# A new order for the pair stage of a spectral mix and gated feed-forward kernel, set by a planner that lets VectorE and POOL take whole turns in SBUF

## The chip, the core and the metric

The kernel runs on one core of a Trainium2 chip. The metric is the device time of one execution in microseconds; the time before is the median of 3 runs, 2704.79 us (2703.63 to 2707.28). The engines are named as in the profile: PE is TensorE, DVE is VectorE, ACT is ScalarE, POOL is GpSimd, SP is SyncE, which here only issues transfers.

## What is computed

```python
# x: 8 x 3008 x 256;  w_r, w_i: 256 x 256;  gate, val: 256 x 1536;  w_out: 1536 x 256
X = np.fft.rfft(x, axis=1)
Yr = Xr @ w_r - Xi @ w_i + b_r
Yi = Xr @ w_i + Xi @ w_r + b_i
Y = soft(Yr) + 1j * soft(Yi)          # soft: sign(v) * max(|v| - 0.01, 0)
y = np.fft.irfft(Y, n=3008, axis=1).reshape(24064, 256)
out = (sigmoid(y @ w_gate) * (y @ w_val)) @ w_out
```

## The kernel before

Every large product is made of three matmuls of parts (high by high, high by low, low by high), so an operand is split into two tiles: ACT writes the rounded part, DVE subtracts it from the value. The transforms and the first columns of the feed-forward end about 1021 us into the profiled execution. What follows to the end is the **pair stage**, the only part that the change touches. It has 19 pairs of column blocks. For each pair it makes both feed-forward products with seven block products in place of eight (Strassen's scheme in Winograd's form), whose intermediate sums are kept in PSUM.

In the code, `half` makes one half (gate or value) of one feature pair: seven products, each of three matmuls of 512 columns (`products`, L1155), into the banks `z`, `c` and `b`. The bank `z` gathers four of the products one after the other, and between two of them ACT copies it out (L1246): a product into `z` must wait for that copy. DVE adds the copies to `b` or `c` (L1249), ACT makes the sigmoid (L1265), and DVE or POOL multiplies gate by value into the tile `h` (L1285, L1287, L1289 on DVE, L1293 on POOL). The multiplication of L1287 frees a `c` bank.

Once three feature pairs are done, `second` makes the output products from `h` into `l2z` banks, again with seven products (of three times three matmuls), again with copies between products (L1351). Its operands are: POOL's differences of slices of `h` (L1320), two sums that a transfer adds into `h` in place (`h<-h`, L1314, issued by POOL, each in two runs of two slices and of one), and the splits of these into tiles `op` (ACT L1331, then DVE L1333). `prepare` loads and splits the next pair's inputs (L1198, L1206, L1207, with POOL's sums at L1211 to L1217). SP issues the loads of weights, `w1s` (L1187, 896 KB, one each half) and `w2s` (L1342, 384 KB, one each product of `second`), and the stores.

The order is a list. Each step is a `Task` with an engine, a duration, a due time and the tasks that it waits for. The due time is the place in a regular scheme plus a number of the table `NUDGE`, one number for each step of each function. `arrange` plays the tasks through a small model of the five engines and the two transfer queues: of the tasks that are ready within `WINDOW` the one with the least due time goes next, and the order in which tasks start there is the order in which the instructions are issued on every engine. On the chip each engine runs its own list strictly in that order. In the model before, a DVE and a POOL step that are both marked `lock` (they work in SBUF alone) run beside each other, each slowed:

```python
both = all(e in busy and busy[e][0].lock for e in SHARED)
rate = {e: SHARED[e] if both and e in SHARED else 1.0 for e in busy}
...
pace = {e: QUEUES[e][0] if len(moving) > 1 else 1.0 for e in moving}
```

Of the kernel before, what the change touches and what calls it, by code (L numbers as in the profile page):

```python
# [112 lines left out]
class Task:  # L113

    def __init__(self, eng, dur, at, fn, deps=(), lat=0.0, lock=False):
# [8 lines left out]
        35.88, 211.51, 46.34, -80.66, 89.38, -188.31, -183.87, 12.03, -179.91, -49.65, -108.66, 69.66, -418.39,  # L124
        -6.25, 526.82, -36.25, 63.45,
    ),
    "half1": (
        30.21, -172.94, -428.44, -29.43, -62.2, -353.59, -143.83, -35.84, -15.75, -266.09, -177.94, -36.82,
        12.27, -36.43, 24.32, -384.25, -231.44,
    ),  # L130
    "last": (
# [5 lines left out]
    ),  # L137
    "load": (
        -3.03,
    ),  # L140
    "prepare": (
        -160.17, 129.89, 132.59, -42.29, -163.88, 148.86, -247.4, 18.25, -9.94, 184.26, 160.89, -45.82, 144.56,
        487.85, -161.32, 91.98, 68.39, -293.04, 78.88,
    ),
# [7 lines left out]
    ),  # L152
# [12 lines left out]
SHARED = {"DVE": 0.47, "POOL": 0.8}  # L165
QUEUES = {"SP": (0.57, 2.06), "POOL": (0.33, 2.48)}
# [9 lines left out]
def arrange(tasks):  # L176
# [3 lines left out]
    queues = {e: [] for e in QUEUES}  # L180
    busy = {}
    for i, t in enumerate(tasks):
# [17 lines left out]
    while len(order) < len(tasks) or busy:  # L200
        wake = []
        for e, ts in waiting.items():
# [15 lines left out]
        step = min(wake + [busy[e][1] / rate[e] for e in busy] + [m[1] / pace[e] for e, m in moving.items()])  # L218
        now += step
        for e, m in moving.items():  # L220
            m[1] -= step * pace[e]
            if m[1] <= 1e-9:
                queues[e].pop(0)
                done(m[0], now + QUEUES[e][1])
        for e in ENGINES:
            if e not in busy:
                continue
            busy[e][1] -= step * rate[e]
            if busy[e][1] > 1e-9:
                continue  # L230
            t = busy.pop(e)[0]
            t.end = now
            if t.lat:
                queues[e].append([t, t.lat])
            else:
                done(t, now)
    return order
# [3 lines left out]
def tile_fft_mix_ffn(ctx: ExitStack, tc, x, w_r, w_i, b_r, b_i, w_one, w_out, mf, mi, mis, fa, ft, out):  # L241
# [866 lines left out]
    def task(eng, dur, at, fn, reads=(), writes=(), lat=0.0, lock=False, deps=()):  # L1108
# [74 lines left out]
    def load_weights(k):  # L1183
# [3 lines left out]
                           lambda: nc.sync.dma_start(t.get().bitcast(F32), td[k // 2 % NH, k % 2]), writes=[t], lat=2.7)  # L1187

    def prepare(p):
# [5 lines left out]
        def part(i, j):  # L1195
# [3 lines left out]
            y.get().rearrange("p t a n -> p t (a n)"), yd[:, :, p * 2 * HW:(p + 1) * 2 * HW]), writes=[y], lat=2.7)  # L1199
# [293 lines left out]
```

## Time and profile before

| what | value |
|---|---|
| median of 3 runs | 2704.79 us (2703.63 to 2707.28) |
| the profiled execution's own time | 2710.75 us |
| its span, from the first to the last instruction | 2708.9 us |
| PE busy over the span | 2662.7 us, 98%, 16763 matmuls |
| DVE, ACT, POOL busy | 79%, 62%, 39% |
| TensorE clock granted over the span | 0.994 of full speed |
| HBM read and written | 440.50 MB and 116.13 MB |

The profiled execution took 5.96 us more than the median of the runs; its rows are used for differences, and these are set against the median. An idle time in the views is the time that an engine stood still before an instruction, with the instruction or transfer that ended it. Since each engine runs its list in order, an instruction that waits holds all those behind it.

### The profile page before, as it was taken

What the parts mean: (1) busy time and instruction counts of PE and PEld (TensorE: products, weight loads), DVE (VectorE), ACT (ScalarE), POOL (GpSimd) and SP (SyncE); (2) the same over time, 40 slices, a digit from 0 to 9 for tenths busy, and PEclk for the clock granted to TensorE, in tenths of its full rate; (3) what the DMA queues carried; (4) which work ended last, traced back from release to release, by engine and by line L of the source; (5) the groups of instructions that cost most, each with busy time, mean ns of one, the idle gap of its engine ahead of it and who ended that gap; (6) DMA issues with size and microseconds to landing.
All of it is one profiled execution on the core that took longest, in us unless ns stands there. A gap on an engine that the chain in (4) does not pass through costs nothing.

```text
span 2708.9 us, 45080 instructions
## 1 busy us (share of the span) xinstructions
PE 2662.7 (98%) x16763; PEld 2178.5 (80%) x16763; DVE 2140.7 (79%) x3100; ACT 1670.5 (62%) x2852; POOL 1055.0 (39%) x963
## 2 busy tenths in 40 slices
PE   9999999999999999999999999999999999999999
PEld 6778888888888878878788788878788788887877
DVE  5778888687789537888888888888888788888876
ACT  4565554545444446676677766766667667776665
POOL 1441012132235013544555445444554455544532
PEclk9999999999999999999999999999999999999999
DMA  9987655677666675878877888787877788787874
GB/s 294 293 285 197 193 151 168 204 208 208 179 185 179 171 218 164 251 237 251 263 238 246 251 246 265 236 247 237 256 249 242 234 269 239 244 259 243 259 227 135
DMA packets 257659, 617.82 MB, mean 228 GB/s; under 512 B 26464, under 2 KB 130656, under 8 KB 257440
## 3 DMA queue, kind: packets, MB, share of 16 engines
q1 hardware_dynamic: 222720, 521.29, 58.5%
q0 software_dynamic: 34608, 93.60, 16.2%
q8 instruction: 133, 2.18, 0.3%
q14 instruction: 86, 0.70, 0.1%
q10 hardware_dynamic: 112, 0.04, 0.0%
HBM read 440.50 MB, written 116.13 MB: 205 GB/s over the span
## 4 chain that ended last, share of the span: by engine, by line
PE 62%; DMA 14%; DVE 10%; ACT 6%; POOL 4%; issue 3%; SPq 0%; DVEq 0%; POOLq 0%; ACTq 0%
PE z L1155 15%; PE l2z L1155 13%; DMA h<-h 11%; PE c L1155 7%; PE pm L447 4%; PE b L1155 3%; PE pb L413 2%; POOL t L1320 2%; PE pia L524 2%; PE pg L577 2%; ACT op L1331 1%; PE pg L578 1%; POOL h L1320 1%; PE po L605 1%; PE pv L577 1%
## 5 line engine op out<-in xcount | busy, mean ns | idle before, releaser
L1155 PE MATMUL z<-xop,w1s 128*128 128x512 f32 x2592 | 684.3, 391 | 11.4 <-ACT tmp L1246 11.1
L1155 PE MATMUL l2z<-op,w2s 128*128 128x512 f32 x2331 | 599.8, 392 | 3.9 <-DMA w2s<-sd 1.9
L1155 PEld LDWEIGHTS z<-xop,w1s 128*128 128x128 f32 x2592 | 484.9, 188 | 123.8 <-ACT tmp L1246 24.0
L1155 PEld LDWEIGHTS l2z<-op,w2s 128*128 128x128 f32 x2331 | 436.2, 188 | 108.2 <-ACT tmp L1351 7.4
L1246 ACT COPY tmp<-z 128x512 f32<-128x512 f32 x684 | 394.3, 584 | 183.1 <-PE z L1155 175.2
L1333 DVE TENSOR_TENSOR op<-h,op 128x1024 fp32r<-128x1024 f32 (+1 forms) x444 | 472.2, 1078 | 24.9 <-ACT op L1331 19.5
L1331 ACT CAST op<-h 128x1024 fp32r<-128x1024 f32 (+1 forms) x444 | 366.4, 837 | 176.1 <-DMA h<-h 100.1
L1155 PE MATMUL c<-xop,w1s 128*128 128x512 f32 x1296 | 362.1, 392 | 5.1 <-DVE h L1287 3.3
L1293 POOL TENSOR_TENSOR h<-tmp 128x512 f32<-128x512 f32 x114 | 180.1, 1580 | 379.6 <-DVE tmp L1249 362.6
L1155 PEld LDWEIGHTS c<-xop,w1s 128*128 128x128 f32 x1296 | 242.7, 188 | 62.8 <-DVE h L1287 10.5
L1249 DVE TENSOR_TENSOR tmp<-tmp,c 128x512 f32<-128x512 f32 x342 | 231.5, 681 | 62.9 <-ACT tmp L1246 41.2
L1320 POOL TENSOR_TENSOR t<-h 128x512 f32<-128x512 f32 x111 | 173.3, 1562 | 158.0 <-DVE h L1285 158.0
L1265 ACT ACTIVATE tmp<-tmp 128x512 f32<-128x512 f32 x342 | 210.3, 632 | 28.4 <-DVE tmp L1249 28.4
L1314 POOL DMA_DIRECT2D h<-h x148 | 128.3, 900 | 165.8 <-DVE h L1289 56.0
L447 PE MATMUL pm<-w_sb,xsh 128*128 128x256 f32 x1008 | 184.4, 285 | 0.0
L1155 PE MATMUL b<-xop,w1s 128*128 128x512 f32 x648 | 182.3, 390 | 0.0
L447 PEld LDWEIGHTS pm<-w_sb,xsh 128*128 128x128 f32 x1008 | 152.9, 189 | 1.0 <-ACT xsh L429 0.4
L1320 POOL TENSOR_TENSOR h<-h 128x512 f32<-128x512 f32 x111 | 148.9, 1341 | 8.7
L458 ACT CAST yh<-yc 128x512 fp32r<-128x512 f32 x84 | 52.2, 621 | 147.0 <-DVE yc L437 146.9
L1155 PEld LDWEIGHTS b<-xop,w1s 128*128 128x128 f32 x648 | 121.3, 188 | 26.0 <-DVE tmp L1249 0.5
L447 PE MATMUL pm<-w_sb,xsl 128*128 128x256 f32 x504 | 139.6, 277 | 0.0
L585 DVE TENSOR_TENSOR sg<-sg,pv 128x512 f32<-128x512 f32 x108 | 74.1, 686 | 74.2 <-PE pv L579 56.0
(199 smaller groups left out, 4933.0 us busy)
## 6 DMA issues: line engine op xcount, KB each, us to landing
w1s<-td SPq DMA_DIRECT2D x228, 896.0 KB, 6.3
w2s<-sd SPq DMA_DIRECT2D x259, 384.0 KB, 4.3
h<-h POOLq DMA_DIRECT2D x74, 512.0 KB, 6.2
zf<-zd SPq DMA_DIRECT2D x96, 256.0 KB, 3.5
vf<-vd SPq DMA_DIRECT2D x128, 192.0 KB, 4.0
vd<-vz SPq DMA_DIRECT2D x84, 256.0 KB, 2.7
ypair<-yd SPq DMA_DIRECT2D x19, 1024.0 KB, 7.4
out_dram<-acc SPq DMA_DIRECT2D x76, 256.0 KB, 4.3
```

What stands on the lines that cost most here:

```text
L447: nc.tensor.matmul(o, l, r, start=(i == 0), stop=(i == len(mms) - 1))
L577: nc.tensor.matmul(t, wh, yth[:, ct], start=(ct == 0), stop=False)
L585: nc.vector.tensor_mul(h, sg, pv)
L1155: nc.tensor.matmul(o, ws[i], vs[j], start=first and not i and not j, stop=i == 1, skip_group_check=not first)
L1246: return t, on("ACT", 0.59, at, lambda: a_.copy(t.get(), z.get()), [z], [t], deps)
L1249: return on("DVE", 0.67, at, lambda: add(t.get(), s.get(), o.get()), [x for x in (s, o) if x is not t], [t], deps)
L1265: return on("ACT", 0.635, at, lambda: a_.activation(t.get(), (o or t).get(), AF.Sigmoid), [o] if o else [], [t], deps)
L1293: made[3, q] = on("POOL", 1.3, 16, lambda: g_.tensor_mul(at_h(3), g22.get(), v.get()), [g22, v], [h], [d22, e22], True)
L1314: return [[on("POOL", 0.9, at + q0, lambda q0=q0, q1=q1: g_.dma_start(h.get()[:, dst, q0:q1], h.get()[:, src, q0:q1], accum_op=ALU.add), [ ...
L1320: return [[on("POOL", 1.3, at + q, lambda q=q: g_.tensor_sub(v()[:, q], h.get()[:, a, q], h.get()[:, b, q]), [h], [o], sum((d[q] for d in ...
L1331: hi = on("ACT", 0.19 + 0.43 * n, at - 8 + q0, lambda q0=q0, q1=q1: a_.copy(t.get()[:, 0, q0:q1], v()[:, q0:q1]), [t_in], [t], sum((d[i] f ...
L1333: lo.append([on("DVE", 0.13 + 0.555 * n, at - 5 + q0, lambda q0=q0, q1=q1: sub(t.get()[:, 1, q0:q1], v()[:, q0:q1], t.get()[:, 0, q0:q1]), ...
```

## The change

The planner's model and the table are changed; no instruction, shape, tile, buffer count or dependence is. Steps that are marked `lock` now run in three phases: 0.147 us in which they run freely, then a wait until the other engine's locked step is done, then the rest. In the queue model each transfer has a length and the share that POOL's transfer gets beside it. The durations of a few steps move by 5 to 15 ns. All numbers of `NUDGE` are new (266 of them); the kernel issues the same instructions in another order.

```diff
 NUDGE = {
     "half0": (
-        35.88, 211.51, 46.34, -80.66, 89.38, -188.31, -183.87, 12.03, -179.91, -49.65, -108.66, 69.66, -418.39,
+        81.78, 197.28, 91.73, -117.95, -250.83, -257.61, -224.48, -163.05, -290.05, -136.01, -349.76, 195.94,
...
-SHARED = {"DVE": 0.47, "POOL": 0.8}
-QUEUES = {"SP": (0.57, 2.06), "POOL": (0.33, 2.48)}
+BEFORE_LOCK = 0.147
+LANDING = {"SP": 2.08, "POOL": 2.13}
+BOTH = 0.848
+W1_LOAD, Y_LOAD, W2_LOAD, OUT_STORE, P_LOAD = (2.58, 0.27), (2.74, 0.39), (1.14, 0.41), (0.83, 0.32), (1.08, 0.6)
+ADDING = (1.82, 0.0), (0.97, 0.0)
...
-            busy[e] = [t, t.dur]
+            busy[e] = [t, BEFORE_LOCK if t.lock else t.dur, 1 if t.lock else 3]
...
-        both = all(e in busy and busy[e][0].lock for e in SHARED)
-        rate = {e: SHARED[e] if both and e in SHARED else 1.0 for e in busy}
         moving = {e: q[0] for e, q in queues.items() if q}
-        pace = {e: QUEUES[e][0] if len(moving) > 1 else 1.0 for e in moving}
+        pool = moving["SP"][0].lat[1] if len(moving) > 1 else 0.0
+        pace = {e: 1.0 if len(moving) < 2 else pool if e == "POOL" else BOTH - pool for e in moving}
...
+            t, _, phase = busy[e]
+            if phase == 1:
+                busy[e] = [t, t.dur - BEFORE_LOCK, 2]
+                continue
+            busy.pop(e)
+            if e in holds:
+                holds.remove(e)
...
+        for e in ENGINES:
+            if e in busy and busy[e][2] == 2 and not holds:
+                busy[e][2] = 3
+                holds.append(e)
```

What the new table makes of the lists is shown at three places. Line numbers of the changed kernel are 14 higher here (L1249 is L1263 there, and so on).

The first is DVE in the second pair, where `second` starts: `op<-t` are splits of POOL's differences in SBUF, `h<-z` and `h<-c` are products of gate and value, and `c<-tmp,c` is the sum that the latter needs. Before:

```order
L1285 TENSOR_TENSOR h<-z,tmp 128x512
L1333 TENSOR_TENSOR op<-t_13922,op 128x1024
L1333 TENSOR_TENSOR op<-t_13922,op 128x512
L1249 TENSOR_TENSOR c<-tmp,c 128x512
L1287 SCALAR_TENSOR_TENSOR h<-c,tmp 128x512
L1249 TENSOR_TENSOR tmp<-tmp,c 128x512
```

The same place in the changed kernel:

```order
L1299 TENSOR_TENSOR h<-z,tmp 128x512
L1347 TENSOR_TENSOR op<-t_13919,op 128x1024
L1263 TENSOR_TENSOR tmp<-tmp,c 128x512
L1263 TENSOR_TENSOR c<-tmp,c 128x512
L1301 SCALAR_TENSOR_TENSOR h<-c,tmp 128x512
L1263 TENSOR_TENSOR tmp<-tmp,c 128x512
L1347 TENSOR_TENSOR op<-t_13919,op 128x512
```

The split of one slice, which stood right ahead of `c<-tmp,c`, now stands four rows later, behind `h<-c`.

The second is ACT in the third pair, around the second of two single casts of `h`: the one that splits a slice into which a transfer has added (`xop` are the next pair's inputs). Before:

```order
L1246 COPY tmp<-z 128x512
L1331 CAST op<-h 128x512 x2
L1206 CAST xop<-s2f 128x512
L1265 ACTIVATE tmp<-z 128x512
L1246 COPY tmp<-z 128x512
L1331 CAST op<-h 128x1024
```

The same place in the changed kernel:

```order
L1345 CAST op<-h 128x512
L1260 COPY tmp<-z 128x512 x2
L1345 CAST op<-h 128x512
L1260 COPY tmp<-z 128x512
L1220 CAST xop<-s2f 128x512
L1279 ACTIVATE tmp<-tmp 128x512 x2
L1345 CAST op<-h 128x1024
```

Two copies of `z` have moved ahead of that cast, and the next copy stands right behind it in place of three rows later.

The third is PE in the fourth pair, two products of one half into one `z` bank (the number behind a name tells the tile, x3 is one product). Before:

```order
L1155 MATMUL z_15279<-xop_15357,w1s_15166 128x512 x3
L1155 MATMUL l2z_15353<-op_15190,w2s_15185 128x512 x3
L1155 MATMUL z_15385<-xop_14638,w1s_15198 128x512 x3
L1155 MATMUL c_15396<-xop_15292,w1s_15198 128x512 x3
L1155 MATMUL z_15279<-xop_15317,w1s_15166 128x512 x3
```

The same two products in the changed kernel:

```order
L1169 MATMUL z_15257<-xop_15337,w1s_15139 128x512 x3
L1169 MATMUL c_15278<-xop_14483,w1s_15119 128x512 x3
L1169 MATMUL l2z_15353<-op_15203,w2s_15190 128x512 x3
L1169 MATMUL z_15257<-xop_15293,w1s_15139 128x512 x3
```

Three products stood between the two before, two stand there now.

## Rows read from the trace of the kernel before

**Rows 1.** Busy time of the engines by stretch, from the start of the pair stage to the end, and in two short stretches: start and end in us, length, busy us of each engine with its count of instructions, granted TensorE clock, share of the DMA engines, GB/s.
```profile
core 0: us, PE busy (x) PEld busy (x) DVE busy (x) ACT busy (x) POOL busy (x), PEclk, DMA share, GB/s
1021.20:2708.90 1687.70, 1663.20 (x7210) 1348.97 (x7208) 1378.99 (x1818) 1155.96 (x1930) 814.22 (x609) 1.00 0.78 240
...
2129.00:2138.00 9.00, 6.82 (x23) 5.12 (x22) 5.53 (x8) 4.31 (x7) 3.54 (x2) 0.81 0.56 172
2612.00:2622.00 10.00, 7.55 (x20) 5.69 (x21) 5.97 (x6) 2.48 (x6) 3.79 (x3) 0.66 0.52 146
```

**Rows 2.** PE in order of time near 1046 us, five products in a row: start us, us, what (128 x 512 outputs, three matmuls), and the stage's end.
```profile
1044.96 0.84 PE L1155 MATMUL z<-s,w1s 128*128 128x512 f32 x3
1045.64 0.84 PE L1155 MATMUL b<-a,w1s 128*128 128x512 f32 x3
...
1048.36 0.84 PE L1155 MATMUL z<-a,w1s 128*128 128x512 f32 x3
...
2701.96 2.88 PE L1155 MATMUL l2z<-op,xop 128*128 128x512 f32 x12
2704.88 0.69 DVE L1444 TENSOR_TENSOR acc<-acc,l2z 128x512 f32<-128x512 f32 x1 [2.03 <-PE l2z L1155]
```

**Rows 3.** Waits of PE's weight loads in the pair stage, whole: who waited for what, us in total, times, longest us.
```profile
PEld z L1155 <- ACT tmp L1246: 24.0, 32, 2.6
PEld c L1155 <- DVE h L1287: 10.7, 18, 0.6
PEld l2z L1155 <- ACT tmp L1351: 7.4, 15, 0.8
PEld l2z L1155 <- DMA w2s<-sd: 7.0, 17, 1.1
PEld c L1155 <- DVE tmp L1249: 2.2, 1, 2.2
PEld l2z L1155 <- DVE acc L1364: 1.4, 4, 0.5
PEld l2z L1155 <- ACT op L1331: 1.1, 1, 1.1
PEld l2z L1155 <- DVE op L1333: 0.7, 1, 0.7
PEld b L1155 <- DVE tmp L1249: 0.5, 2, 0.4
PEld b L1155 <- issue: 0.5, 2, 0.3
PEld z L1155 <- DMA w1s<-td: 0.4, 1, 0.4
```

**Rows 4.** The engines in order of time in the second pair, 1143.9 to 1150.9 us: start us, us, engine and what, idle time before it and what ended it.
```profile
1143.93 0.69 DVE L1285 TENSOR_TENSOR h<-z,tmp 128x512 f32<-128x512 f32 x1 [0.41 <-PE z L1155]
1144.41 0.84 PE L1155 MATMUL b<-xop,w1s 128*128 128x512 f32 x3
1144.54 1.22 DVE L1333 TENSOR_TENSOR op<-t,op 128x1024 fp32r<-128x1024 f32 x1
1144.61 0.59 ACT L1246 COPY tmp<-z 128x512 f32<-128x512 f32 x1 [0.42 <-PE z L1155]
...
1146.98 1.29 POOL L1320 TENSOR_TENSOR h<-h 128x512 f32<-128x512 f32 x1
1147.13 0.84 PE L1155 MATMUL c<-xop,w1s 128*128 128x512 f32 x3
...
1147.59 1.24 DVE L1333 TENSOR_TENSOR op<-t,op 128x512 fp32r<-128x512 f32 x1 [1.83 <-ACT op L1331]
...
1148.74 0.68 DVE L1249 TENSOR_TENSOR c<-tmp,c 128x512 f32<-128x512 f32 x1
...
1149.46 0.69 DVE L1287 SCALAR_TENSOR_TENSOR h<-c,tmp 128x512 f32<-128x512 f32 x1
...
1150.21 0.96 PE L1155 MATMUL c<-xop,w1s 128*128 128x512 f32 x3 [0.20 <-DVE h L1287]
...
1150.84 0.69 DVE L1333 TENSOR_TENSOR op<-h,op 128x512 fp32r<-128x512 f32 x1
```

**Rows 5.** The same view in the third pair, 1283.4 to 1293.3 us.
```profile
1283.47 0.82 POOL L1314 DMA_DIRECT2D h<-h  x1
...
1291.10 0.62 ACT L1331 CAST op<-h 128x512 fp32r<-128x512 f32 x1 [1.93 <-DMA h<-h]
...
1291.62 0.61 ACT L1206 CAST xop<-s2f 128x512 fp32r<-128x512 f32 x1
1292.14 0.59 ACT L1265 ACTIVATE tmp<-z 128x512 f32<-128x512 f32 x1
...
1292.63 0.58 ACT L1246 COPY tmp<-z 128x512 f32<-128x512 f32 x1
...
1293.26 0.98 PE L1155 MATMUL z<-xop,w1s 128*128 128x512 f32 x3 [0.28 <-ACT tmp L1246]
```

**Rows 6.** Transfers: the first row is of all 148 sums that a transfer adds into `h` (L1314), the second of the `w2s` loads (L1342) of the whole stage, the third of the two `w2s` loads between 1414.2 and 1420 us. Each gives the time from issue to landing.
```profile
DMA to landing us min/median/max: 3.3/6.4/12.9
...
DMA to landing us min/median/max: 2.7/4.3/11.5
...
DMA to landing us min/median/max: 9.1/9.4/9.6
```

**Rows 7.** The longest wait of ACT that a transfer ended, in the pair stage, columns as in Rows 3.
```profile
ACT op L1331 <- DMA h<-h: 100.1, 55, 4.1
```

More of the change, by code (lines that the diff above doesn't have):

```diff
@@ L113, with __init__ @@
 class Task:
-    def __init__(self, eng, dur, at, fn, deps=(), lat=0.0, lock=False):
+    def __init__(self, eng, dur, at, fn, deps=(), lat=None, lock=False):
         self.eng, self.dur, self.at, self.fn, self.lat, self.lock = eng, dur, at, fn, lat, lock
@@ L179, in arrange @@
     waiting = {e: [] for e in ENGINES}
-    queues = {e: [] for e in QUEUES}
+    queues = {e: [] for e in LANDING}
     busy = {}
+    holds = []
     for i, t in enumerate(tasks):
@@ L210, in arrange @@
             ts.remove(t)
-            busy[e] = [t, t.dur]
+            busy[e] = [t, BEFORE_LOCK if t.lock else t.dur, 1 if t.lock else 3]
             t.start = now
             order.append(t)
-        both = all(e in busy and busy[e][0].lock for e in SHARED)
-        rate = {e: SHARED[e] if both and e in SHARED else 1.0 for e in busy}
         moving = {e: q[0] for e, q in queues.items() if q}
-        pace = {e: QUEUES[e][0] if len(moving) > 1 else 1.0 for e in moving}
-        step = min(wake + [busy[e][1] / rate[e] for e in busy] + [m[1] / pace[e] for e, m in moving.items()])
+        pool = moving["SP"][0].lat[1] if len(moving) > 1 else 0.0
+        pace = {e: 1.0 if len(moving) < 2 else pool if e == "POOL" else BOTH - pool for e in moving}
+        step = min(wake + [b[1] for b in busy.values() if b[2] != 2] + [m[1] / pace[e] for e, m in moving.items()])
         now += step
@@ L223, in arrange @@
                 queues[e].pop(0)
-                done(m[0], now + QUEUES[e][1])
+                done(m[0], now + LANDING[e])
         for e in ENGINES:
-            if e not in busy:
+            if e not in busy or busy[e][2] == 2:
                 continue
-            busy[e][1] -= step * rate[e]
+            busy[e][1] -= step
             if busy[e][1] > 1e-9:
                 continue
-            t = busy.pop(e)[0]
+            t, _, phase = busy[e]
[5 more added lines that the diff above has]
+                holds.remove(e)
             t.end = now
             if t.lat:
-                queues[e].append([t, t.lat])
+                queues[e].append([t, t.lat[0]])
             else:
                 done(t, now)
+        for e in ENGINES:
+            if e in busy and busy[e][2] == 2 and not holds:
+                busy[e][2] = 3
+                holds.append(e)
     return order
@@ L1106, in get, with task @@
             return self.ap
-    def task(eng, dur, at, fn, reads=(), writes=(), lat=0.0, lock=False, deps=()):
+    def task(eng, dur, at, fn, reads=(), writes=(), lat=None, lock=False, deps=()):
         kind, i = here
@@ L1198, in prepare @@
         ld = task("SP", 0.45, (base + 1) * SLOT, lambda: nc.sync.dma_start(
-            y.get().rearrange("p t a n -> p t (a n)"), yd[:, :, p * 2 * HW:(p + 1) * 2 * HW]), writes=[y], lat=2.7)
+            y.get().rearrange("p t a n -> p t (a n)"), yd[:, :, p * 2 * HW:(p + 1) * 2 * HW]), writes=[y], lat=Y_LOAD)
         def sum_(at, fn, out, reads, deps):
-            return task("POOL", 1.3, (base + at) * SLOT, fn, reads=reads, writes=[out], deps=deps, lock=True)
+            return task("POOL", 1.295, (base + at) * SLOT, fn, reads=reads, writes=[out], deps=deps, lock=True)
         def split(name, at, src, v, deps):
@@ L1248, in summed @@
         def summed(at, t, s, o, deps):
-            return on("DVE", 0.67, at, lambda: add(t.get(), s.get(), o.get()), [x for x in (s, o) if x is not t], [t], deps)
+            return on("DVE", 0.685, at, lambda: add(t.get(), s.get(), o.get()), [x for x in (s, o) if x is not t], [t], deps)
         q1 = prod(0, z, "a11", "b11", True)
@@ L1288, in half @@
         d11 = summed(3.5, b, s, b, [ds, q2])
[L1289 removed]
+        made[0, q] = on("DVE", 0.685, 4.6, lambda: mul(at_h(0), g11.get(), b.get()), [g11, b], [h], [d11, e11])
         v = new_tmp()
@@ L1314, in sum_ @@
             return [[on("POOL", 0.9, at + q0, lambda q0=q0, q1=q1: g_.dma_start(
-                h.get()[:, dst, q0:q1], h.get()[:, src, q0:q1], accum_op=ALU.add), [h], [], sum((d[i] for d in deps), []), lat=0.6 if i else 1.85)]
+                h.get()[:, dst, q0:q1], h.get()[:, src, q0:q1], accum_op=ALU.add), [h], [], sum((d[i] for d in deps), []), lat=ADDING[i])]
                 for i, (q0, q1) in enumerate(RUNS)]
         def difference(at, o, v, a, b, deps):
-            return [[on("POOL", 1.3, at + q, lambda q=q: g_.tensor_sub(v()[:, q], h.get()[:, a, q], h.get()[:, b, q]),
+            return [[on("POOL", 1.295, at + q, lambda q=q: g_.tensor_sub(v()[:, q], h.get()[:, a, q], h.get()[:, b, q]),
                         [h], [o], sum((d[q] for d in deps), []), True)] for q in range(FG)]
@@ L1361, in result @@
             if s:
-                before = [on("POOL", 1.3, at - 1, lambda: g_.tensor_add(t.get(), t.get(), s.get()), [s], [t],
+                before = [on("POOL", 1.295, at - 1, lambda: g_.tensor_add(t.get(), t.get(), s.get()), [s], [t],
                              before + list(deps[:1]), True)]
-            d = on("DVE", 0.67, at, lambda: add(t.get(), t.get(), o.get()), [o], [t], [*deps, *before])
+            d = on("DVE", 0.685, at, lambda: add(t.get(), t.get(), o.get()), [o], [t], [*deps, *before])
             ct, s_ = divmod(j, 2)
             col = T0 + (2 * p + s_) * HW
-            on("SP", 0.45, at + 2, lambda: nc.sync.dma_start(out[ct * P:(ct + 1) * P, col:col + HW], t.get()), [t], [], [d], lat=1.2)
+            on("SP", 0.45, at + 2, lambda: nc.sync.dma_start(out[ct * P:(ct + 1) * P, col:col + HW], t.get()), [t], [], [d], lat=OUT_STORE)
             return d
```

39 lines of the change are left out of this document (19 added, 20 removed), and 37 rows, old and new, of the table NUDGE.

## The prediction

> **What bounds the kernel now.** I read the busy times by stretch first. The pair stage lasts 1687.7 us, holds 7210 matmuls, and the clock is granted in full over it [rows 1]. Then PE in order of time: products of three matmuls start 0.68 us apart, five of them in the 3.40 us from 1044.96 to 1048.36 [rows 2]. So 7210 matmuls need 7210 / 3 x 0.68 = 1634 us. The last product group starts at 2701.96, holds four products and has issued them by 2704.7; about 4 us of the stage are the last sums and stores behind it [rows 2]. That leaves 1687.7 - 1634 - 4 = 49 to 50 us in which PE could have issued and did not. **This is the ceiling of any reordering: 1.8% of the time.** PE's matmuls are neither removed nor shortened, so PE stays the bound.
>
> Next I asked who those microseconds waited for. The waits of PE's weight loads sum to 55.9 us in 94 waits [rows 3]; each holds some 0.04 us that stands before every load anyway (0.227 us from load to load, of which about 0.19 is the load), so 52 us of loss, near the 49 to 50 by counting. The reader is to see that four rows carry 49.1 of the 55.9: `z` on ACT's copies 24.0, `c` on a DVE product 10.7, `l2z` on ACT's copies 7.4, `l2z` on a transfer of weights 7.0 [rows 3]. Transfers name themselves in the last only, but they stand behind the first too, as the next part shows.
>
> A further part of the loss is clock. In 2129 to 2138 us the granted clock was 0.81 on average, in 2612 to 2622 it was 0.66, against 1.00 over the stage [rows 1]. Both stretches lie behind a pause of PE of about 2 us (the longest waits of 2.6 and 2.2 us) [rows 3]. If the clock was at its lower level, 1.2 of 2.4 GHz, for a part of each, those parts are 9 x 0.38 = 3.4 us and 10 x 0.68 = 6.8 us long; PE does half of its work there, less the pause that fell in, so about 4.5 us are lost.
>
> **Term 1, the lock: -10 us.** In the second pair, POOL's difference ran from 1146.98 to 1148.27. DVE's split of one slice began at 1147.59 and took 1.24 us, while the same form took 0.69 us at 1150.84 with POOL idle [rows 4]. It ended 0.56 us behind POOL's end, so it stood still for most of POOL's turn and then ran at full speed: whole turns, not two slowed steps. Behind it stood `c<-tmp,c` (1148.74) and `h<-c` (1149.46), and PE's next product into that `c` bank started at 1150.21, having waited for `h<-c` [rows 4]. This is the row `c` on DVE L1287, 10.7 us in 18 waits, nearly one in each pair [rows 3]. In the new list that split stands behind `h<-c`. Counted along both lists: of the places where only three products separate the product that fills a `c` bank from the next into it, 20 had a locked DVE step right ahead of the sum before, and none has now. Bounds: 0 to -10.7; I take -10, since the wait has no other cause in the rows. Its cover if I am wrong is the one product of slack that the new places have, 0.68 us. The split itself is late next, but its user, an `l2z` product, lies nine or more products on.
>
> **Term 2, `z` on ACT's copies: -10 us.** The third pair shows the mechanism. POOL issued a sum at 1283.47; ACT's cast of the slice started at 1291.10, the transfer having ended its wait of 1.93 us; then a cast, a sigmoid and the copy followed in ACT's list, and PE's `z` product started at 1293.26 behind the copy [rows 5]. ACT waits 100.1 us for such sums [rows 7], and copies that stand behind a waiting cast inherit it. Between a product into `z` and the next one into the same bank there must be room for the copy: the copy starts 0.20 us after its product's slot ends (1144.61 against 1144.41) and lasts 0.59 [rows 4], so with 0.05 to the next product about 0.85 us, which two products (1.36 us) cover with 0.5 to spare. A chain is exposed if it has only two products and its copy stands within three rows behind a cast that waits for a sum. Counted along the lists, 106 of 684 chains were exposed and 61 are, and right behind such a cast 53 and 9. I price an exposed chain from the row, 24.0 / 106 = 0.23 us; 45 fewer give -10.2. Bounds: -24, and above nothing, for there are more thin chains in all (the third rival).
>
> **Term 3, `l2z` on ACT's copies: -1 us.** The same share of 7.4 us [rows 3] would go, -3.1. But eight of these copies now have one product to hide behind, 0.68 us, where about 0.85 is needed [rows 2, 4]; with a restart of PE of about 0.1 that is 8 x 0.27 = +2. Bounds -7 to +2.
>
> **Term 4, weights for `l2z`: 0.** 7.0 us in 17 waits [rows 3]. The load for the fifth product in the first half of a pair had 14 products (9.5 us) between the release of its buffer and its use; it has 9 or 10 now, 6.1 to 6.8 us. In the order before it was issued right behind a `w1s` load, and two such loads landed 9.1 and 9.6 us after issue; but the median of all is 4.3 [rows 6]. In SP's new list one `w1s` load that stood ahead stands behind it, so I expect near 6.5 us: some waits go, some come. Bounds: -7, and if every one of 19 landed at 9.1 as before, 19 x 2.6 = +49.
>
> What the DMA engines can give is a limit here: they are busy 0.78 of the stage [rows 1], and a transfer beside others takes long: POOL's sums land between 3.3 and 12.9 us after issue [rows 6]. The Trainium skill (DMA: Bandwidth & Descriptors, section Issuing engines are not separate DMA queues) says that transfers issued from different engines end up on the same 16 DMA engines and interleave. By that rule moving a transfer only moves its delay, terms 2 to 4 would come to 0 and the sum would be that of the first rival below; the trace agrees that transfers slow each other, but it also has a sum that landed in 3.3 us.
>
> **Term 5, clock: -2 us.** Without pauses of 2 us the 4.5 us above go; I take half, as late transfers can still make one. Bounds -4.5 to +4.5.
>
> SP's and POOL's own lists are permuted too, and nothing is added to them: their instructions cost PE nothing while the four rows above stay the waits. Stages ahead of 1021 us keep their order, and the last pair's tail keeps its shape: 0 for both.
>
> **Sum:** -10 - 10 - 1 + 0 - 2 = -23 us. The profiled execution took 2710.75 us, 5.96 more than the median of the runs; I set the difference against the median: 2704.8 - 23 = **2682 us**, own range 2671 to 2693.
>
> **Rivals.** *Transfers keep PE waiting:* POOL's sums and weight loads land as late in the new order; only the lock goes. For it: the DMA share of 0.78, and the longest sum of 12.9 us [rows 1, 6]. Against: casts are seldom right ahead of thin chains now. Time: 2704.8 - 10 = 2695 us.
>
> *Waits change places:* the new list is as full as the old, and for each wait gone another comes; the planner's gain stays in the planner. For it: the old list was set by a planner as well, and 49 us were left. Against: the old planner ran locked steps side by side, which the rows of the second pair contradict [rows 4]. Time: 2701 to 2708 us.
>
> *Thin chains, slower:* the list has 302 `z` chains with only two products where it had 179 of 684. Such a chain has 0.5 us to spare, less than one cast of 0.62 us on ACT [rows 5]. If ACT falls behind its planned place by over 0.5 us, whatever for, each may stall PE. Price: 24.0 us over 179 chains is 0.134 us each; 123 more without the relief of term 2 are +16.5, with the two restarts and falls of the clock that such pauses brought, 4.5 once more, +21. Less the lock's 10 this is 2704.8 + 11 = 2716 us. Against it: 73 of the old thin chains stood away from waiting casts, and the cases that I followed were not among them. The point that decides is ACT's lag against that half microsecond.
>
> *Nearly all goes:* only 4 to 5 us of the 49 remain: 2704.8 - 44 = 2661 us. Against it: transfers vary from one execution to the next.
>
> **Chances.** Forecast 0.50; transfers keep PE waiting 0.16; waits change places 0.11; thin chains 0.15; nearly all 0.08. About 0.2% (5.4 us) is what a measurement of this kernel can tell from no change. Faster by more: 0.50 + 0.16 + 0.08 = 0.74. Within: 0.11. Slower: 0.15, where the high bound of term 4 lies too. The range leaves out the slower case and about 0.05 of the last one, and holds the bounds of terms 1 to 3 and 5: 2663 to 2708 us.
>
> **What would show it.** Term 1: the row `c` on DVE L1301 falls from 10.7 to under 2 us. Term 2: `z` on ACT L1260 falls to about 14 us, with fewer waits of ACT for `h<-h` right before a copy. Term 3: `l2z` on L1365 stays at 5 to 8. Term 4: `l2z` on `w2s` stays near 7 and is not the first row. Term 5: no stretch of the stage with a clock under 0.9. The sum: the waits of PE's weight loads come to 30 to 36 us in place of 55.9, and the stage to about 1665. A row `z` on ACT L1260 above 30 us means the thin chains; a `w2s` row above 20 us means that term 4 was at its high end. A stage that shortens by more than the fall of these rows would make the whole reading wrong.

## The result, and the profile after

| kernel | median us | ratio to before, 95% interval | waits of PE's weight loads in the pair stage, summed |
|---|---|---|---|
| before | 2707.16 (6 runs) | 1 | 55.9 us |
| changed | 2721.20 (6 runs) | 1.0063 [1.0048, 1.0078] | 70.7 us |

The change costs 0.63%, 14 to 17 us, where 23 us of gain were forecast. The profiled execution's span is 2720.1 us, 11.2 longer than before. In the first rows the columns are those of [rows 1]:

```profile
1017.20:2720.10 1702.90, 1659.47 (x7210) 1348.08 (x7208) 1451.40 (x1818) 1170.55 (x1930) 828.00 (x608) 1.00 0.77 238
1340.00:1345.00 5.00, 4.76 (x14) 3.77 (x15) 1.79 (x3) 3.22 (x6) 0.00 (x0) 0.66 0.06 24
1698.00:1703.00 5.00, 4.87 (x14) 3.85 (x15) 1.85 (x3) 3.15 (x6) 0.00 (x0) 0.66 0.12 49
```

PE issues the same matmuls, but the stage is 15.2 us longer, and DVE shows 72 us more busy time for the same 1818 instructions: time in which its steps stand still, as the split in [rows 4] did. Next the waits of PE's weight loads, as in [rows 3], and ACT's row of [rows 7]:

```profile
PEld z L1169 <- ACT tmp L1260: 25.4, 18, 3.2
PEld c L1169 <- DVE tmp L1263: 19.9, 25, 2.3
PEld l2z L1169 <- DVE op L1347: 11.6, 8, 1.6
PEld l2z L1169 <- DMA w2s<-sd: 4.3, 7, 0.8
PEld c L1169 <- DVE h L1301: 3.4, 9, 0.8
PEld l2z L1169 <- ACT tmp L1365: 3.4, 8, 0.4
```

```profile
ACT op L1345 <- DMA h<-h: 42.2, 21, 4.3
```

The rows that the prediction wanted smaller are smaller, except `z`: fewer waits (18 for 32), yet each 1.4 us in place of 0.75. And two rows that were nearly nothing before, `c` on DVE's sums (2.2) and `l2z` on DVE's splits (0.7), now hold 31.5 us.

I followed each late product of PE back, instruction by instruction, to the first cause, and summed what PE lost there (us over the stage):

| first cause | before | after |
|---|---|---|
| a sum that a transfer adds into `h` landed late | 19.3 | 18.5 |
| a DVE step stood for POOL's turn in SBUF | 8.7 | 25.5 |
| loads of weights and of the next pair's inputs | 4.3 | 5.5 |

So the sums cost the same as before, in nine late products, 1.2 us and more each, in place of some 36 that were mostly under 0.7, and the turns, which the new planner was to know better, cost three times as much. The rows hold 32.3 of some 49 us that PE lost in the stage before, and 49.5 of some 64 after (start to start, over 0.227 us a matmul). The rest, 17 and 15 us, lies in PE's restarts, the stretches of lowered clock and short waits.

**The late sum.** In every second pair one place looks like this (second pair, in order of time):

```profile
1149.87 0.85 POOL L1328 DMA_DIRECT2D h<-h  x1 [3.58 <-DVE op L1347]
1150.09 0.33 SPq L1201 DMA_DIRECT2D w1s<-td  x1
...
1159.82 0.62 ACT L1345 CAST op<-h 128x512 fp32r<-128x512 f32 x1 [4.11 <-DMA h<-h]
1160.34 1.06 ACT L1260 COPY tmp<-z 128x512 f32<-128x512 f32 x2
...
1161.46 0.50 PE L1169 MATMUL z<-xop,w1s 128*128 128x512 f32 x1 [2.56 <-ACT tmp L1260]
```

POOL issues the sum, SP 0.2 us later an 896 KB load; the sum lands 9.9 us after its issue, ACT's cast stands for it, the two copies stand behind the cast, and PE stands behind the second copy, into whose bank its next `z` product goes. Nine such places, 1.2 to 2.9 us each, are 18 of the 18.5 us in the first row of the table. Behind two of them (2.9 and 2.5 us) the granted clock was at its lower level, 1.2 GHz: products start 1.28 us apart in place of 0.68. Behind two others (2.7 and 2.6 us) it was not.

```profile
1341.12 1.48 PE L1169 MATMUL c<-xop,w1s 128*128 128x512 f32 x3
1342.40 1.48 PE L1169 MATMUL z<-xop,w1s 128*128 128x512 f32 x3
1343.68 0.63 PE L1169 MATMUL b<-xop,w1s 128*128 128x512 f32 x1
```

**The long turn.** A DVE split of 128x512 takes 0.69 us alone. Here it takes 3.15 us, and a ready sum (`tmp<-tmp,c`; its last input was there at 1186.9, when a copy of ACT ended) stands behind it and PE behind that:

```profile
1191.24 1.75 POOL L1328 DMA_DIRECT2D h<-h  x2
...
1191.72 3.15 DVE L1221 TENSOR_TENSOR xop<-ypair,xop 128x512 fp32r<-128x512 f32 x1
...
1192.39 1.93 POOL L1225 TENSOR_TENSOR s1f<-ypair 128x512 f32<-128x512 f32 x1
...
1194.80 0.67 DVE L1263 TENSOR_TENSOR tmp<-tmp,c 128x512 f32<-128x512 f32 x1
...
1195.53 0.51 PE L1169 MATMUL c<-xop,w1s 128*128 128x512 f32 x1 [1.09 <-DVE tmp L1263]
```

The split starts 0.67 us *before* POOL's step by the records, while POOL issues a transfer (the row holds two issues, one after the other), and yet it ends 0.56 us behind that step. In the kernel before, a split waited over 1.2 us, longer than a plain turn, three times (1.9 us each); here 31 times, up to 2.7 us. In all 34 an issue of POOL stands right ahead of the POOL step. A second place of this kind, 6 us later in the same pair, feeds `l2z` (7 times, some 1.3 us of PE each):

```profile
1197.71 0.86 POOL L1328 DMA_DIRECT2D h<-h  x1 [1.70 <-DVE op L1347]
1197.92 3.07 DVE L1347 TENSOR_TENSOR op<-h,op 128x1024 fp32r<-128x1024 f32 x1
1198.31 1.58 POOL L1226 TENSOR_TENSOR s2f<-s1f,ypair 128x512 f32<-128x512 f32 x1
...
1201.04 1.21 PE L1169 MATMUL l2z<-op,w2s 128*128 128x512 f32 x4 [1.10 <-DVE op L1347]
```

### The profile page after: what moved, and what is told of

Same layout as the page of the kernel before. It is cut to its first block, busy times and chain, and to the rows that moved or that the text cites. A ratio compares the mean times of both kernels' runs of the same rounds, so it can differ in the third digit from the quotient of the medians.

```text
span 2720.1 us, 45230 instructions
## 1 busy us (share of the span) xinstructions
PE 2655.1 (98%) x16763; PEld 2175.2 (80%) x16763; DVE 2212.4 (81%) x3100; ACT 1684.6 (62%) x2852; POOL 1071.3 (39%) x963
## 4 chain that ended last, share of the span: by engine, by line
PE 69%; DVE 13%; DMA 10%; issue 4%; ACT 2%; POOL 2%; SPq 0%; DVEq 0%; POOLq 0%; ACTq 0%
PE z L1169 18%; PE l2z L1169 15%; PE c L1169 9%; DMA h<-h 5%; PE b L1169 5%; PE pm L461 4%; PE pb L427 2%; DMA ypair<-yd 2%; PE pia L538 2%; PE pg L591 1%; DVE op L1347 1%; PE pa L327 1%; DVE ys L468 1%; DMA w2s<-sd 1%; PE pg L592 1%
## 5 line engine op out<-in xcount | busy, mean ns | idle before, releaser
L1169 PE MATMUL l2z<-op,w2s 128*128 128x512 f32 x2331 | 610.1, 391 | 9.9 <-DVE op L1347 8.1
L1347 DVE TENSOR_TENSOR op<-h,op 128x1024 fp32r<-128x1024 f32 (+1 forms) x444 | 521.9, 1187 | 55.8 <-ACT op L1345 53.2
L1169 PEld LDWEIGHTS l2z<-op,w2s 128*128 128x128 f32 x2331 | 435.9, 188 | 110.8 <-DVE op L1347 11.6
L1169 PE MATMUL c<-xop,w1s 128*128 128x512 f32 x1296 | 361.8, 393 | 10.8 <-DVE tmp L1263 10.4
L1263 DVE TENSOR_TENSOR tmp<-tmp,c 128x512 f32<-128x512 f32 x342 | 232.0, 681 | 27.6 <-ACT tmp L1260 12.7
L1334 POOL TENSOR_TENSOR t<-h 128x512 f32<-128x512 f32 x111 | 162.4, 1463 | 145.6 <-DVE h L1299 127.6
L1334 POOL TENSOR_TENSOR h<-h 128x512 f32<-128x512 f32 x111 | 188.3, 1696 | 7.9
```

The costliest lines, as they stand in the source:

```text
L1169: nc.tensor.matmul(o, ws[i], vs[j], start=first and not i and not j, stop=i == 1, skip_group_check=not first)
L1263: return on("DVE", 0.685, at, lambda: add(t.get(), s.get(), o.get()), [x for x in (s, o) if x is not t], [t], deps)
L1334: return [[on("POOL", 1.295, at + q, lambda q=q: g_.tensor_sub(v()[:, q], h.get()[:, a, q], h.get()[:, b, q]), [h], [o], sum((d[q] for d i ...
L1347: lo.append([on("DVE", 0.13 + 0.555 * n, at - 5 + q0, lambda q0=q0, q1=q1: sub(t.get()[:, 1, q0:q1], v()[:, q0:q1], t.get()[:, 0, q0:q1]), ...
```

## Experiments

All but two kernels take one of the two finished lists and move single steps in it; no step is added, removed or given to another engine. A step is named by its function and number there (`("second0", 32)` is the 33rd step of the first `second` of a pair, `half0` and `half1` are the two halves). A row says which step goes behind or ahead of which other, where that stands at most so many rows away on the same engine:

```diff
-        for t in arrange(tasks):
+        for t in moved(arrange(tasks)):
```

The medians were taken on several chips; compare the ratios, each against the kernel before on the same chip.

| kernel | median us | ratio, 95% interval | PE's load waits, us |
|---|---|---|---|
| e1_cast_later | 2699.78 | 0.9996 [0.9984, 1.0007] | 51.6 |
| e2_dve_sums_first | 2714.82 | 1.0062 [1.0038, 1.0086] | 59.2 |
| e3_issue_behind | 2712.24 | 1.0039 [1.0025, 1.0054] | 55.1 |
| e4_all_three | 2698.88 | 0.9983 [0.9970, 0.9995] | 42.8 |
| e5_load_later | 2692.82 | 0.9967 [0.9957, 0.9977] | 52.3 |
| e6_four | 2683.93 | 0.9936 [0.9919, 0.9953] | 34.3 |
| e7_five | 2681.18 | 0.9922 [0.9907, 0.9937] | 26.7 |
| b1_split_later | 2702.61 | 1.0005 [0.9992, 1.0018] | 59.0 |
| b2_casts_later | 2686.79 | 0.9947 [0.9929, 0.9964] | 37.7 |
| b3_both | 2683.56 | 0.9935 [0.9917, 0.9952] | 38.1 |

### The late sum: e1_cast_later and e5_load_later

```diff
+MOVES = ((("second0", 32), "behind", ("half0", 7), 2),)
```

> The changed kernel with one move: in every second pair ACT's cast that waits for the late sum (the high part of the slice summed last but one in the first half) stands behind the two z copies that stood behind it; 9 moves, all else as in the changed kernel (2721.2 us). Theory A, late sum: the 9 pauses of PE ahead of one z product (1.2 to 2.9 us, 18.5 us together) come from that cast alone and go; with them the two falls of the clock at 1340 and 1699 us. The row z on ACT's copies (L1260) falls from 25.4 us to 5 to 9, ACT's cast still waits for its sum, and nothing else grows by over 3 us, because the cast's users stand far behind: 2698 to 2704 us. Rival, thin chains (two products between one z product and the next into its bank, whatever stands ahead of the copy): the row stays above 18 us and the time above 2714. Rival, full list: the row falls as in theory A, but the cast's late user or the next wait takes its place, l2z on DVE or ACT grows by 10 us or more, and the time stays within 5 us of 2721.

Nine moved casts take 0.67% off the changed kernel (1.0063 to 0.9996), 18 us. The waits, as above:

```profile
PEld c L1169 <- DVE tmp L1263: 17.4, 27, 1.6
PEld l2z L1169 <- DVE op L1347: 14.1, 13, 1.6
PEld l2z L1169 <- ACT tmp L1365: 6.5, 12, 1.1
...
PEld z L1169 <- ACT tmp L1260: 2.8, 5, 1.4
```

The row `z` fell from 25.4 to 2.8, lower than expected; the `l2z` rows on DVE and ACT grew by 5.6 together, too little for the full list. All the chains with two products between one `z` product and the next into its bank are still in this list, and where no waiting cast stands ahead of the copy they cost at most the 2.8 us that are left: the rival of the thin chains is refuted.

```diff
+MOVES = ((("load", 0), "behind", ("second0", 63), 1),)
```

> The changed kernel with one move on SP alone: in every second pair the w1s load that is issued 0.2 us behind the late sum stands behind the w2s load that followed it (10 moves), so that it is issued some 4 us later; the cast that waits for the sum stays ahead of the z copies. Theory, the sum is late because that load's transfer goes beside it: the sum lands 2 us or more sooner (8.4 to 10.0 us from issue to landing now, under 7.5 then), the nine pauses of PE (18.5 us) fall under 8 us, time -10 to -14: ratio to the kernel before 1.001 to 1.003. Rival, the two w2s loads ahead of it and POOL's own two sums ahead in its queue make it late: it lands as late as now within 0.7 us, the row z on ACT's copies stays above 20 us, ratio above 1.004. If the load then comes too late for its product, z on w1s shows it.

One load in every second pair, issued some 4 us later against the sum (in the second pair 3.9 us behind the sum's issue in place of 0.2), made the kernel 26 us faster (1.0063 to 0.9967). The place of the late sum, second pair again:

```profile
1149.19 0.85 POOL L1328 DMA_DIRECT2D h<-h  x1 [4.32 <-DMA h<-h]
...
1153.11 1.47 SPq L1201 DMA_DIRECT2D w1s<-td  x1
...
1154.35 0.62 ACT L1345 CAST op<-h 128x512 fp32r<-128x512 f32 x1
```

With the load so much later the sum lands 5.1 us after issue instead of 9.9; over the eight later pairs of this kind 5.4 to 7.9 where 7.7 to 10.0 had been. The cast finds it there, and the row `z` is 3.7 us. No row for the late load appeared. The gain is larger than expected and larger than e1's by 0.29%, which the load waits (52.3 and 51.6) do not explain; the profiled execution of e5 was the slowest of its ten (2700.73 against a median of 2692.82), so its rows may overstate what is left. That part stays open.

### The long turn: e2_dve_sums_first and e3_issue_behind

```diff
+MOVES = ((("half0", 11), "ahead", ("prepare", 4), 2),)
```

> The changed kernel with one move: in 8 of the 17 pairs that prepare the next pair's operands, DVE's sum of tmp and c (half0's, L1263), which had been ready for 4 to 8 us, stands ahead of the locked split of the operand (xop from ypair) instead of behind it. Theory B, long lock: that split waits 1.3 to 2.5 us because POOL holds the turn from a DMA issue on to the end of the locked step behind it, and PE's product into c inherits it; the split's wait stays, the row c on DVE tmp (L1263) falls from 19.9 us to 8 to 11, and the time by 10: 2709 to 2713 us. Rival, DVE is simply too full (81% busy): the wait moves to DVE's next sums, the row stays above 15 us or l2z on DVE rows grow by as much, and the time stays within 4 us of 2721.

The row `c` fell by 7.4 us, to 12.5, and no DVE row grew:

```profile
PEld c L1169 <- DVE tmp L1263: 12.5, 16, 1.5
PEld l2z L1169 <- DVE op L1347: 10.1, 7, 1.6
```

The time does not settle it: four runs from 2711.5 to 2725.7, an interval of 0.5%. What remains in the row is mostly a later sum of the same half (step 15 of `half0`), behind which PE loses 0.5 to 1.2 us in seven of these pairs.

```diff
+MOVES = ((("second1", 25), "behind", ("prepare", 2), 1),)
```

> The changed kernel with one move on POOL alone: in 8 pairs the issue of the second half's last sum stands behind the locked step that followed it (sum and difference of ypair) instead of ahead. No locked step is added or taken, only the issue no longer stands right ahead of that step. Theory B, long lock: DVE's split of 1.24 us that waited 1.83 us in 7 of these pairs for that step waits at most a plain turn (1.1 us) or not at all; the 7 pauses of 1.38 us of PE inside one l2z pair of products go; the row l2z on DVE's split (L1347) falls from 11.6 us to 1 to 4, and the time by 7 to 10: 2711 to 2714 us. Rival, the locked step alone makes the wait, with or without an issue ahead of it: the split still waits 1.2 to 1.9 us, the row stays above 8 us, and the time stays within 3 us of 2721. What may come against both: the sum is issued about 1.3 us later, and ACT's cast behind it may wait that much longer.

```profile
PEld c L1169 <- DVE tmp L1263: 20.1, 22, 1.6
...
PEld l2z L1169 <- DVE op L1347: 0.8, 1, 0.8
```

With only the issue moved behind the step the row fell from 11.6 to 0.8, the time by 0.24%, 6.5 us. So the order, issue and then step, makes this stall. That the issue lengthens the turn is not shown by this run, for the step no longer meets the split at all:

```profile
1197.27 1.29 POOL L1226 TENSOR_TENSOR s2f<-s1f,ypair 128x512 f32<-128x512 f32 x1
...
1199.64 1.81 DVE L1347 TENSOR_TENSOR op<-h,op 128x1024 fp32r<-128x1024 f32 x2
```

In the changed kernel the issue had waited 1.70 us for a DVE split and held POOL's step up behind it; here the step runs at once and ends 1.07 us before the split begins, in all 8 pairs. Whether the issue itself adds to a turn is the question of the small kernel below.

### How the parts add: e4_all_three, e6_four, e7_five

> The changed kernel with all three moves of the runs before: cast behind the z copies, DVE's sum ahead of the operand's split, issue behind the locked step. If the three causes are separate, as theories A and B have it, their gains add: -20, -10 and -9 us, 2721.2 - 39 = 2682 us (2678 to 2690), below the kernel before (2707.2) by 0.9%; the waits of PE's weight loads sum to about 36 us. If waits change places (the list is full, each wait that is taken away lets the next one show), the sum falls short of the parts by half or more: 2700 us or above.

22 us of the 39 came. Alone the three moves had given 18, 0 and 6.5 us, so most of what is missing was missing from the parts; what they do give nearly adds. The largest row now is `c` on DVE's sums, 22.4 us, and its place is new:

```profile
1194.82 1.27 POOL L1226 TENSOR_TENSOR s2f<-s1f,ypair 128x512 f32<-128x512 f32 x1
1194.94 1.70 DVE L1347 TENSOR_TENSOR op<-h,op 128x512 fp32r<-128x512 f32 x1
1196.57 0.67 DVE L1263 TENSOR_TENSOR tmp<-tmp,c 128x512 f32<-128x512 f32 x1
...
1197.29 0.50 PE L1169 MATMUL c<-xop,w1s 128*128 128x512 f32 x1 [1.83 <-DVE tmp L1263]
```

POOL's step, no longer behind the issue, now runs when another split is due, a plain turn of 1.0 us, and again a ready sum stood behind that split. So here a wait did take the place of another, and it could be moved too:

```diff
 MOVES = (
     (("second0", 32), "behind", ("half0", 7), 2),
     (("half0", 11), "ahead", ("prepare", 4), 2),
     (("second1", 25), "behind", ("prepare", 2), 1),
+    (("second1", 13), "behind", ("half0", 15), 1),
 )
```

> The three moves of the run before and a fourth: in the same 8 pairs DVE's locked split of a slice (second half, tmp to op) stands behind the sum of h and c that PE's product half0 (fifth of the half) waits for. In the run before that split lost the turn to POOL (1.7 us in place of 0.69) with this sum behind it, and PE stood 1.5 to 2.2 us at this product in 8 pairs (16.7 us with four stalls further on, and 5 us of lowered clock behind them). Theory, the wait only shows because a ready sum stands behind a locked step: the row c on DVE (22.4 us) falls to about 8, the stage's loss from 41.5 to 22 to 28 us, the time by 14 to 18 us, to a ratio of 0.991 to 0.993 of the kernel before. Rival, every wait taken away lets the next one show: the loss stays above 36 us and the ratio above 0.997.

Ratio 0.9936, 13 us better than e4_all_three, the row `c` at 10.8: a little short of the 14 to 18 us and of the 8 us foretold, and far from the rival. With the load of e5 as a fifth move:

> The changed kernel with all five moves: those of the run with four, and the w1s load behind the w2s load on SP. The stage's loss was 26.7 us with four; what the load can still take away is the rest behind the late sum (1.4 us at an l2z product, 1.2 us of lowered clock, parts of the restarts). If the two cures of the late sum overlap, as the theory has it, the gain over the run with four is 1 to 5 us, ratio 0.992 to 0.9935, and not the 26 us that the load alone was worth. If the load's move also shortens other transfers, the loss falls under 20 us and the ratio under 0.991.

```profile
PEld l2z L1169 <- DVE op L1347: 6.4, 9, 0.8
PEld c L1169 <- DVE tmp L1263: 5.6, 12, 0.9
PEld z L1169 <- ACT tmp L1260: 3.7, 8, 0.8
```

The five moves, 43 steps of some 7300, beat the kernel before by 0.78% and the changed one by 1.4%; no wait is over 1.2 us, and no products 1.28 us apart are left in the stage. The two cures of the late sum overlap, as expected: the load is worth 4 us here, which the intervals of the two runs do not tell from nothing, and 26 alone.

### The prediction's terms alone, in the old list: b1, b2, b3

```diff
+MOVES = ((("second0", 19), "behind", ("half1", 16), 2),)
```

> The kernel before with the first part of the change alone, in 17 pairs: DVE's locked split of 1.24 us that stood ahead of the sums into tmp and h stands behind the second of them. Term 1 of the prediction (-10 us) says that the row c on DVE h (L1287) falls from 10.7 us to under 2 and the time by about 10. Counted at PE's products the stalls behind that split are 6.1 us and some 2 us of restarts, so the reading of after gives -6 to -8: ratio 0.997 to 0.998. Rival, the wait goes elsewhere (the l2z product that uses the split, or DVE's sums behind it): the row falls, another DVE row grows by 4 us or more, and the ratio is above 0.999.

```profile
PEld z L1155 <- ACT tmp L1246: 30.5, 41, 2.0
PEld c L1155 <- DVE tmp L1249: 9.2, 18, 2.2
...
PEld c L1155 <- DVE h L1287: 0.2, 1, 0.2
```

The 10.7 us of term 1 are gone and nothing is won: a `c` product now waits 0.4 us for DVE's sum into tmp in each of the same 17 pairs, and `z` waits 6.5 us more (late products of PE that begin with a late sum: 44, and 36 before). The rival has it.

```diff
+MOVES = ((("second1", 22), "behind", ("half0", 7), 3), (("second0", 32), "behind", ("half0", 7), 2))
```

> The kernel before with the idea of term 2 alone: ACT's two casts that wait for a late sum (one in each half of a pair, 18 and 17 moves) stand behind the z copy of half0 that stood behind them. Term 2 priced what the new order would do at -10 us of the row z on ACT's copies (L1246, 24.0 us). By PE's products the stalls at that copy are 7.2 us in the second half and about 5 in the first, with some 3 us of restarts: the row falls from 24.0 to 6 to 10 us and the time by 10 to 15, ratio 0.9945 to 0.996. Rival, transfers keep PE waiting: the cast, now later on ACT, hands its wait to the copies of the next chains or to l2z; the row stays above 16 us or l2z rows grow by 8, ratio above 0.998.

> The kernel before with both edits, 52 moved instructions and the rest of the old order kept: if terms 1 and 2 of the prediction were right as mechanisms and add, -16 to -22 us, ratio 0.992 to 0.994, about what was forecast for the change (-23). If gains shown apart are not to be had together, above 0.996.

The casts alone give 0.53%, 14 us (row `z` from 24.0 to 2.2), both edits 0.65%, 18 us. So term 2's mechanism is sound, and the lock is worth some 3 us once the casts no longer bind, less than the intervals of the two tell apart.

### The turn by itself: m1_turns and m2_turns

The small kernel's loop, where `width` sets DVE's distance from POOL's start (16 to 1024 columns of an ACT copy; in two of the eight distances the two copies change places and are equally wide):

```python
a_.copy(go[:, 1, :16], p[:, :16])              # wait for POOL's last sum
a_.copy(go[:, 1, 16:32], acc[:, 0, :16])       # and for the last transfer
a_.copy(go[:, 0, :64], src[:, :64])            # starts POOL
a_.copy(late[:, :width], src[:, :width])       # starts DVE
if slices:
    g_.dma_start(acc[:, :slices], go[:, :slices], accum_op=ALU.add)
if op:
    g_.tensor_add(p, go[:, 0], src[:, :512])
v_.tensor_sub(d, late[:, :512], src[:, :512])
```

> A kernel by itself that computes nothing of the reference: one DVE subtraction in SBUF (128x512), started by an ACT copy at eight set distances from POOL's start, 4 times each, in five cases: POOL idle (tile d_alone), POOL with one sum in SBUF (d_op), POOL with one issue of an adding transfer of two slices (d_issue), POOL with an issue of one or of two slices and the sum right behind it (d_issue1_op, d_issue2_op). Theory of the held turn: about 0.69 us in the first and third case whatever the distance; up to 0.69 + 1.1 us in the second when DVE starts inside the sum; in the last two also when DVE starts during the issue, so up to 0.69 + 1.9 with an issue of one slice and 0.69 + 2.7 with two, ending about 0.56 us behind POOL's sum. Rival, the turn is taken only when the sum itself begins: DVE steps that start during the issue end after 0.69 us and none lasts over 0.69 + 1.2 us. Second rival, the issue itself holds DVE: steps of the third case last 1.2 us or more.

The program's scheduler moved the instructions of m1, so POOL and DVE did not meet at the set distances, and nothing is read from it. With the order fixed:

```diff
+    with tc.manual_schedule():
         for case, slices, op in CASES:
```

> The small kernel again, computing nothing of the reference, with its instructions kept in the order written (in the run before they were reordered, and POOL and DVE did not meet at the set distances). Five cases of 32 DVE subtractions (128x512 in SBUF), at eight distances from POOL's start each. Theory of the held turn: 0.69 us throughout in d_alone and d_issue; in d_op up to 0.69 + 1.1 us when DVE starts inside POOL's sum; in the two cases with an issue and a sum right behind it, DVE steps that start during the issue also stand until POOL's sum ends, up to 0.69 + 2 us and more, ending 0.56 us behind it. Rival, the turn is taken only when the sum itself begins: a DVE step that starts 0.7 us or more ahead of the sum's recorded start ends after 0.69 us, and none lasts over 0.69 + 1.2 us.

Means of DVE's step by case, and two of the runs with an issue:

```profile
L292 DVE TENSOR_TENSOR d_issue_op<-late,src 128x512 f32<-128x512 f32 x64 | 82.6, 1291 | 228.5 <-ACT late L287 161.4 <-ACT late L283 67.0
L292 DVE TENSOR_TENSOR d_op<-late,src 128x512 f32<-128x512 f32 x32 | 31.8, 994 | 35.9 <-ACT late L287 23.0 <-ACT late L283 12.9
L292 DVE TENSOR_TENSOR d_issue<-late,src 128x512 f32<-128x512 f32 x32 | 22.1, 692 | 150.0 <-ACT late L287 114.0 <-ACT late L283 35.9
L292 DVE TENSOR_TENSOR d_alone<-late,src 128x512 f32<-128x512 f32 x32 | 22.1, 691 | 18.8 <-ACT late L287 15.6 <-ACT late L283 3.2
```

```profile
348.78 0.69 DVE L292 TENSOR_TENSOR d_issue_op<-late,src 128x512 f32<-128x512 f32 x1 [3.33 <-ACT late L287]
348.82 0.89 POOL L289 DMA_DIRECT2D acc<-go  x1 [1.85 <-ACT late L287]
349.43 1.58 POOL L291 TENSOR_TENSOR p<-go,src 128x512 f32<-128x512 f32 x1
...
381.37 0.88 POOL L289 DMA_DIRECT2D acc<-go  x1 [1.84 <-ACT go L286]
381.63 2.47 DVE L292 TENSOR_TENSOR d_issue_op<-late,src 128x512 f32<-128x512 f32 x1 [1.53 <-ACT late L287]
381.98 1.56 POOL L291 TENSOR_TENSOR p<-go,src 128x512 f32<-128x512 f32 x1
```

An issue alone costs DVE nothing in 32 of 32 cases. With a sum behind it, a DVE step that starts 0.35 us ahead of the sum's recorded start takes 2.47 us and ends 0.56 behind the sum. Over all distances the steps that start up to 0.50 us ahead are held (2.62 us the longest), those that start 0.51 ahead or more take 0.69; in both fences the issue's record begins some 0.6 us ahead of the sum's, so nearly the whole issue is held. The rivals fall: the longest wait is 1.9 us, over the 1.2 of the first, and the issue by itself makes none. (That a step which starts 0.7 us or more ahead is free, as the first rival says, is so; the theory's limit was the start of the issue, and it is 0.1 us inside it.) A sum without an issue held DVE 1.0 us at most. The waits of up to 2.7 us in the changed kernel, behind two issues in a row, are longer than any here (a split that starts 0.85 us ahead of the step is still held there); two issues in a row were not tried in the small kernel.

## Why the prediction was wrong

Set beside the table of first causes, the turns were to give 10 us and cost 17, and the late sums were to give 10 and gave 1. Both terms failed, and the turns make the larger part of the miss.

**Term 1 (-10) was right in its row, and its step to the time failed.** The row `c` on DVE L1301 fell by 7.3 us, to 3.4, not under 2. The wrong step is the count of "20" places where a locked DVE step stood ahead of the sum "before, and none has now": it looked only at the places where the old list lost turns, and put what the new list loses at other places at nothing. There, turns longer than the 1.3 us of [rows 4] cost 17 us more: 31 waits of over 1.2 us in place of 3, each with POOL's issue ahead of its step. The new model cannot see them, since an issue of POOL is a step of 0.9 us without `lock` in it and a DVE step that starts beside it counts as free; no run tests a planner that knows better. Nor was "the wait has no other cause in the rows" enough for -10: b1 shows that this wait alone was worth nothing, since the sum or the copy next in line was nearly as late.

**Term 2 (-10, came as +1.4 in its row) failed in its price.** The counts come out of the lists as stated. The wrong step is "I price an exposed chain from the row, 24.0 / 106 = 0.23 us". The chains are not alike. Of the 61 exposed chains in the new list nine, one in every second pair, have their copy second behind a cast whose sum lands 8 to 10 us after issue, and pay 18 / 9 = 2.0 us each. They were counted, and priced at 2 us together. The other 52 show no late product that begins with a sum, and the nine that the term counted right behind such a cast are among these 52. The casts that wait in the second half (7.2 of the 19.3 us before) were cured indeed. The lateness was to be had beforehand too: the new list has an 896 KB load next to that issue, and [rows 6] had a sum of 12.9 us. Term 2 took the sums' lateness as unchanged and asked only who stands behind them. The planner's model priced this too low as well: it gives POOL's transfer 0.27 of its speed beside that load, so the sum takes 0.97 / 0.27 = 3.6 us in place of 0.97. That is an estimate of 2.6 us more, where the traces have 4.8 more (9.9 against 5.1).

**Term 3** came out at -4.0 (expected -1), **term 4** at -2.7 (expected 0): both within their bounds. **Term 5** (-2): two stretches of lowered clock as before, nothing gained. The bounds of terms 1 to 3 and 5 add to 2659 to 2711 us, a little more than the 2663 to 2708 that was said to hold them; 2721 lies outside either.

The signs named beforehand: the `z` row stayed under 30 us and `w2s` under 20, so neither of the two warnings spoke; the sum of the load waits (30 to 36 foretold, 70.7 found) and the stage (1665, 1702.9) did. Of the rivals the thin chains gave the nearest time, 2716 us, by a mechanism that e1 refutes; "waits change places" is the nearest in kind, with b1 and e4 as its cases, but not as a law, for e6 and e7 show that the list was not full. "Transfers keep PE waiting" had the cause of 18.5 of the 49.5 us that the table holds after the change. There I let a rule of the Trainium skill (DMA: Bandwidth & Descriptors, section Issuing engines are not separate DMA queues) stand for more than it says: transfers of different engines do interleave, and the trace agrees (9.9 us with the load right behind the sum, 5.1 with it later). That moving one only moves its delay was my addition, and e5 refutes it: the load had 4 us to spare, as no row of waits for it appeared, and the sum had none.

## What to carry over

Price a wait at its own place, from the lateness of the thing waited for and what stands right behind it, never by a mean over places that look alike; then ask of each moved transfer which short transfer it now runs beside. In a queue that runs in order, put ready work ahead of whatever may have to wait, and take a planner's order as a draft: here a trace of it and 43 moved steps won more than twice what the change had lost.

## What the runs showed of the hardware

POOL's step queued behind a DMA issue keeps DVE's two-input steps in SBUF out before its own recorded start: in m2 from 0.5 us ahead of it, with up to 1.9 us of wait for a 1.27 us step, whose record is then 1.55 to 1.6 us long. The Trainium skill (SBUF — State Buffer, section Who interferes with whom) says that a DVE step with two SBUF inputs contends with a POOL step that reads SBUF, that the port is an exclusive lock, and that issue order decides who blocks. The case d_op agrees (up to 1.69 us when DVE starts 0.12 us behind, 0.69 when it starts first); with an issue ahead, the one that seems to start first by the records lost.

A 256 KB adding transfer took 9.9 us with an 896 KB load issued 0.2 us behind it and 5.1 us with the load 3.9 us behind (nine places: 7.7 to 10.0 and 5.1 to 7.9 us), while the load itself could spare the time.
